# Sorted-block attention and its feed-forward: the first half of a hand-written order listed anew, one call per engine, with first keys in four PSUM tiles

## The chip, the core and the metric

One NeuronCore of a Trainium2 chip runs the whole program in one launch. The metric is the device time of that launch in microseconds (us). The engines named below are PE (TensorE, the matrix products; PEld is its loading of weights), DVE (VectorE), ACT (ScalarE), POOL (GpSimd) and SP (SyncE, which here only starts transfers). Each engine works through its own list of instructions in order. An instruction waits on semaphores until what it reads is written and what it overwrites is no longer needed, and all that stands behind it in the same list waits too. Transfers started from POOL run on a software queue (q0 in the profile), those started from SP on a hardware queue (q1).

## The reference, cut to what matters

```python
# q, k, v: (4, 8, 768, 64); sort_net: (4, 8, 8, 8); 8 blocks of 96 tokens
P = sort_net
for _ in range(5):                      # Sinkhorn rounds
    P = P - max(P, -1); P = exp(P)
    P = P / (sum(P, -1) + 1e-9); P = P / (sum(P, -2) + 1e-9)
k_sorted = einsum('bhij,bhjcd->bhicd', P, k_blocks)   # the same for v
scores = 1/8 * q_blocks @ k_sorted.T                  # block by block, 96 x 96
attn = exp(scores - max); attn /= sum(attn) + 1e-9
x = (attn @ v_sorted) as (3072, 512)
h = x @ w_in                                          # w_in (512, 2048)
out = (h * cos(h)) @ w_out                            # w_out (2048, 512)
```

## The kernel before

The work is cut into 8 chunks `n` of 384 tokens. A chunk is half of one batch entry: 4 blocks `u` of 96 tokens, all 8 heads. For each chunk the kernel turns the queries so that the head dimension lies on the partitions, multiplies them with the sorted keys (scores `sc`), takes the row maximum and subtracts it (DVE lines 492, 494, 824, 828), takes the exponential (ACT, line 573, into `p_buf`), turns the result (`pT`, by PE or by a DMA transpose from SP, line 591), multiplies with the sorted values (`av`, line 628), normalises (lines 639, 641) and turns into `xT`. Then comes the feed-forward: `up` (PE, line 672, 8 pairs of feature tiles in PSUM tiles `h`), cosine (ACT, line 676), gate `c * h` (DVE, line 680), and the output layer `down` (PE, line 697, PSUM tiles `o`), whose result is copied out and stored from SP (line 687).

The sorted keys and values come from products of the loaded `k`, `v` with block-diagonal matrices `bd`, `bdv` that are spread from the Sinkhorn result. Batches 0 and 1 are sorted at the beginning (`kp`, `v0`, `v_sort_b`), batches 2 and 3 in the middle (`k_sort_g`, `v_sort_g`). PSUM tiles come from two pools, `big` (handed on as `*B`) and `acc` (`*C`).

Nothing schedules the work: the order is a hand-written list of calls, and each call issues instructions on one or more engines. Each engine's list is the order in which these calls name it. `fill=` puts products of zeros (line 246) ahead of a call's own products on PE.

The transfers that matter below:

- `load_q(n)` starts from POOL. For n of 3 and more it is 8 transfers of 48 KB in pieces of 128 bytes (line 129), and `q_transpose_dma(n)` then turns them with two DMA transposes from SP into `q_turned` (line 149). Chunks 0 to 2 are turned by PE.
- `load_pair(vbuf, ...)`, z from 0 to 5, loads the values of batches 2 and 3 in six transfers of 256 KB from POOL (line 92). `v_permute` is a copy on POOL that reorders values (line 179).
- `p_hold(2, 2)` is a tiny copy on POOL that reads `pT` of block (2, 2), so that POOL waits there until that DMA transpose has landed (line 599). `hold_keys()` does the same for the swapped keys (line 429), `hold(q_turned[z])` for queries.
- `k_swap(kT[1])` moves sorted keys between partitions with two transfers from SP (lines 421, 422).

The first use of chunk 3's queries is `batch(("sc", 3, 0), ("ks", 1, A))`, a set of 8 score products (line 507) and 16 key products on PE.

Of the kernel before, what the change touches and what calls it, by code (L numbers as in the profile page):

```python
# [18 lines left out]
def kernel(  # L19
# [377 lines left out]
    blocks = [block([pick[:]])]  # L397
    spread(bds[0], blocks[0], xs=slice(H, 2 * H))

    def values_matrix():  # L400
        spread(bdv, blocks[1], xs=slice(0, H))
        spread(bds[0], blocks[0], xs=slice(0, H))
        spread(bdv, blocks[1], xs=slice(H, 2 * H))
# [197 lines left out]
    def p_hold(n, u):  # L601
        hold(pT[n, u])
# [14 lines left out]
    def av_products(n, u, fill=0):  # L617
# [5 lines left out]
        pt = pT.pop((n, u)).rearrange("p a c -> p (a c)")  # L623
# [270 lines left out]
    wz = iter(range(40, D, 4))  # L894
    kz = iter(range(6, 12))

    def k_next():
        k_sort_g(next(kz) * 4, A, *C)

    def w_next(eng=A, pool=None, tag="acc"):  # L900
        v_sort_g(next(wz), 4, eng, pool or acc, tag)

    kp(2, *B)
    kp(0, *B)
    v_permute(slice(0, 64), 32, False, 8, 40)
    v_permute(slice(0, 64), 40, False, 8, 48)
    v_permute(slice(0, 64), 48, False, 8, 56)
    v_permute(slice(0, 64), 56, False, 8, 64)
    k_place(2, A, 1)
    k_place(2, V, 0)  # L910
    kp(1, *B)
    k_place(0, A, 0)
    blocks.append(block([pick[:, :, z * PB:(z + 1) * PB] for z in (1, 0)]))
    k_place(1, V, 0)
    k_place(1, A, 1)
    values_matrix()
    k_place(0, A, 1)
    s_ps(0, 0, fill=3)
    v0(4, *C)
    s_max(0, 0)  # L920
    v0(0, *B)
    v0e(4, A)
    s_sub(0, 0)
    s_ps(0, 3)
    v0e(0, A)
    v0(5, *C)
    s_max(0, 3)
    load_w_out(0)
    v0e(5, A)
    s_ps(0, 1)  # L930
    load_w_out(1)
    load_w_out(2)
    load_w_out(3)
    v0(6, *C)
    ones(0)
    expo(0, 0, True)
    s_ps(0, 2)
    s_sub(0, 3)
    v0(1, *C)
    v0e(6, A)  # L940
    s_max(0, 1)
    expo(0, 3, True)
    v0(3, *B, fill=2)
    s_sub(0, 1)
    v0e(1, A)
    p_ps(0, 0, *C, fill=2)
    v0e(3, A)
    s_max(0, 2)
    v0(7, *C)
    expo(0, 1, True)  # L950
    kxp(2)
    v0(2, *B, fill=1)
    p_ev(0, 0, V)
    v0e(7, A)
    s_sub(0, 2)
    kxp(0)
    p_ps(0, 1, *C)
    v0e(2, A)
    p_ps(0, 3, *C)
    p_ev(0, 1, V)  # L960
    expo(0, 2, True)
    kxp(1)
    av_products(0, 0)
    z_turned(1)
    av_norm(0, 0, True)
    av_products(0, 1)
    p_ev(0, 3, A)
    p_ps(0, 2, *C)
    av_norm(0, 1, True)
    x_ps(0, 0, *B)  # L970
    load(kbuf, 0, kin_d[1])
    p_ev(0, 2, A)
    load(vbuf, 64, vin_d[1])
    picks(pick_pair, (2, 3))
    av_products(0, 3, fill=2)
    av_norm(0, 3, True)
    x_ps(0, 1, *C)
    x_ev(0, 0, A)
    av_products(0, 2)
    q_products(1, 0, 0, 16, *C)  # L980
    x_ev(0, 1, A)
    av_norm(0, 2, True)
    x_ps(0, 3, *B)
    q_place_half(1, 0, 1, A)
    up_four(0, 0, 0)
    z_vperm()
    up_four(0, 0, 1)
    x_ev(0, 3, V)
    q_place_half(1, 0, 0, V)
    up_four(0, 3, 0)  # L990
    up_four(0, 3, 1)
    z_turned(0)
    cos_four(0, 0)
    p_pads()
    up_four(0, 1, 0)
    cos_four(0, 3)
    gate_four(0, 0)
    x_ps(0, 2, *C)
    up_four(0, 1, 1)
    gate_four(0, 3)  # L1000
    up_four(0, 2, 0)
    cos_four(0, 1)
    up_four(0, 2, 1)
    x_ev(0, 2, V)
    gate_four(0, 1)
    up_four(1, 2, 0)
    cos_four(0, 2)
    up_four(1, 2, 1)
    gate_four(0, 2)
    up_four(1, 1, 0)  # L1010
    cos_four(1, 2)
    up_four(1, 1, 1)
    gate_four(1, 2)
    up_four(1, 3, 0)
    cos_four(1, 1)
    up_four(1, 3, 1)
    gate_four(1, 1)
    q_products(1, 1, 0, 16, *C)
    cos_four(1, 3)
    last = block([pick_pair[:]], *C)  # L1020
    q_place_half(1, 1, 0, V)
    up_four(1, 0, 0)
    q_place_half(1, 1, 1, A)
    gate_four(1, 3)
    up_four(1, 0, 1)
    s_ps(1, 1)
    spread(bds[1], last)
    cos_four(1, 0)
    s_ps(1, 0)
    s_max(1, 1)  # L1030
    down_four(0, 0)
    gate_four(1, 0)
    load_q(2)
    down_four(0, 1)
    load_pair(pair, kin_d, 0 * CD // 2, 1 * CD // 2)
    load_pair(pair, kin_d, 1 * CD // 2, 2 * CD // 2)
    v_permute(slice(64, 128))
    down_four(0, 2)
    s_sub(1, 1)
    down_four(1, 0)  # L1040
    s_max(1, 0)
    expo(1, 1, True)
    ks(5, *B)
# [211 lines left out]
```

## Time and profile before

| what | us |
|---|---|
| median of 3 runs | 232.06 (231.93 to 232.34) |
| the profiled execution | 231.61 |
| its span in the profile | 229.8 |
| PE busy | 220.8 (96%) |
| DVE, ACT, POOL busy | 170.8, 154.4, 96.1 |
| PE on the chain that ended last | 90% of the span |

The span runs from the first to the last instruction that the profile shows; 1.8 us of the profiled execution lie outside it. The chain that ended last is found by going back from the last instruction, at each step to what released it. An idle row such as `[12.68 <-DMA pT<-p_buf]` says how long the engine stood still just before that instruction, and what ended it. "DMA to landing" is the time from the issue of a transfer to its completion.

### The profile page before, as it was taken

To read this page: it belongs to the slowest core of one execution; us is meant where nothing else is said; L and a number is where in the kernel's file an instruction comes from. 1 tells how busy PE (TensorE), PEld (TensorE's weight loads), DVE (VectorE), ACT (ScalarE), POOL (GpSimd) and SP (SyncE) were. 2 spreads that over 40 slices of the span, in tenths; PEclk is the share of its full clock that TensorE was granted. 3 is DMA by queue.
4 is the path that set the end of the run, shared out by engine and by line. 5 is a ranking of instruction groups with operands and counts; after the bars stand their busy time and mean duration, and the time that the engine had idled before them with its cause. 6 is when DMAs were issued, how large, how long until landed. Compare 5 with 4: busy or idle time off the path is not lost.

```text
span 229.8 us, 5513 instructions
## 1 busy us (share of the span) xinstructions
PE 220.8 (96%) x2245; PEld 138.7 (60%) x2268; DVE 170.8 (74%) x291; ACT 154.4 (67%) x207; POOL 96.1 (42%) x121
## 2 busy tenths in 40 slices
PE   8788999999999999999999999999999999999994
PEld 3378898567765566655665456655655565556554
DVE  6769968978698778868489977987699769646700
ACT  5659877777889858797688466736674667716521
POOL 7999999399950197943609000800000000000000
PEclk9999999999999999999999999999999999999999
DMA  6999999994999799667979939964924440351012
GB/s 83 225 187 207 202 206 236 195 227 148 124 124 191 171 139 148 118 135 146 162 118 163 135 74 148 210 98 81 206 92 80 90 160 0 69 147 46 0 46 94
DMA packets 67833, 31.21 MB, mean 136 GB/s; under 512 B 56416, under 2 KB 63200, under 8 KB 67552
## 3 DMA queue, kind: packets, MB, share of 16 engines
q0 software_dynamic: 24048, 13.64, 43.3%
q1 hardware_dynamic: 43472, 17.02, 35.1%
q8 instruction: 18, 0.29, 0.5%
q10 hardware_dynamic: 288, 0.20, 0.3%
q14 instruction: 7, 0.06, 0.1%
HBM read 27.27 MB, written 6.29 MB: 146 GB/s over the span
## 4 chain that ended last, share of the span: by engine, by line
PE 90%; DVE 3%; POOL 2%; issue 1%; ACT 1%; POOLq 0%; ACTq 0%
PE h L672 32%; PE o L697 30%; PE h L860 5%; PE o L881 4%; PE av L628 4%; PE sc L441 3%; PE ks L408 2%; PE o L1219 2%; PE pps L838 1%; PE sc L507 1%; PE xps L659 1%; PE vs L785 1%; PE vs L452 1%; PE qps L268 1%; PE xps L847 1%
## 5 line engine op out<-in xcount | busy, mean ns | idle before, releaser
L672 PE MATMUL h<-xT,w_in_t 128*128 128x384 bf16 x448 | 78.4, 326 | 0.1
L697 PE MATMUL o<-w_out_t,gg 128*128 128x512 bf16 x303 | 73.7, 379 | 1.0 <-issue 0.3
L676 ACT ACTIVATE c<-h,half_pi 128x768 f32<-128x768 f32 x56 | 50.5, 902 | 26.0 <-PE h L672 25.0
L680 DVE TENSOR_TENSOR gg<-c,h 128x768 bf16<-128x768 f32 x56 | 52.7, 949 | 19.5 <-ACT c L676 19.5
L672 PEld LDWEIGHTS <-w_in_t 128*128 128x128 bf16 x448 | 42.2, 98 | 26.3 <-DVE xT L259 0.6
L697 PEld LDWEIGHTS <-gg 128*128 128x128 bf16 x320 | 29.0, 99 | 28.3
L573 ACT ACTIVATE p_buf<-s 96x768 bf16<-96x768 f32 x32 | 26.6, 843 | 5.2 <-DVE s L494 4.0
L179 POOL COPY vperm<-kv 64x768 bf16<-64x768 bf16 (+2 forms) x12 | 28.4, 2416 | 3.9 <-DMA kv<-in_v_dram 3.9
L494 DVE TENSOR_TENSOR s<-sc,mx 96x384 f32<-96x384 f32 (+1 forms) x33 | 24.3, 735 | 1.6
L492 DVE TENSOR_REDUCE mx<-sc 96x4 f32<-96x384 f32 (+1 forms) x33 | 24.0, 729 | 0.2 <-PE sc L507 0.2
L641 DVE TENSOR_TENSOR xn<-av,r 96x512 bf16<-96x512 f32 x32 | 22.0, 687 | 1.1
L129 POOL DMA_DIRECT2D kv<-in_q_dram x24 | 16.0, 676 | 0.7 <-issue 0.7
L257 ACT COPY kv<-o 128x512 f32<-128x512 f32 (+2 forms) x10 | 5.2, 524 | 14.1 <-PE o L697 11.5
L257 ACT CAST kTs<-ks 128x512 bf16<-128x512 f32 (+1 forms) x18 | 11.0, 630 | 5.3 <-PE ks L408 4.4
L639 DVE RECIPROCAL r<-av 96x8 f32<-96x8 f32 x32 | 6.4, 199 | 9.6 <-PE av L628 9.1
L129 POOL DMA_DIRECT2D q_mem<-in_q_dram x16 | 10.7, 687 | 2.0 <-DMA kv<-in_v_dram 1.5
L881 PE MATMUL o<-w_out_t,gg 128*128 128x512 bf16 x45 | 11.2, 379 | 0.2
L259 DVE COPY kv<-o 128x512 f32<-128x512 f32 (+1 forms) x5 | 3.1, 612 | 11.1 <-PE o L1219 8.5
L860 PE MATMUL h<-xT,w_in_t 128*128 128x192 bf16 x128 | 11.1, 246 | 0.0
L441 PE MATMUL sc<-kTs,q_turned 128*128 128x96 bf16 x152 | 11.1, 206 | 0.0
L599 POOL CAST held<-q_turned 96x1 f32<-96x1 bf16 x2 | 0.4, 184 | 24.3 <-DMA q_turned<-q_mem 16.3
L860 PEld LDWEIGHTS <-w_in_t 128*128 128x128 bf16 x128 | 10.5, 98 | 0.0
(134 smaller groups left out, 285.6 us busy)
## 6 DMA issues: line engine op xcount, KB each, us to landing
out_dram<-kv SPq DMA_DIRECT2D x12, 256.0 KB, 2.7
out_dram<-o_s SPq DMA_DIRECT2D x10, 256.0 KB, 3.5
w_in_t<-in_moe_w_in_dram POOLq DMA_DIRECT2D x4, 512.0 KB, 11.7
w_out_t<-in_moe_w_out_dram POOLq DMA_DIRECT2D x4, 512.0 KB, 12.3
kv<-in_k_dram POOLq DMA_DIRECT2D x2, 768.0 KB, 9.8
kv<-in_v_dram POOLq DMA_DIRECT2D x2, 768.0 KB, 12.9
pair<-in_k_dram POOLq DMA_DIRECT2D x2, 768.0 KB, 12.3
kv<-in_v_dram POOLq DMA_DIRECT2D x6, 256.0 KB, 5.3
```

The costliest lines, as they stand in the source:

```text
L129: nc.gpsimd.dma_start(out=q_heads[:, i, :, e], in_=src[:, ih * IC + i, :, e])
L179: nc.gpsimd.tensor_copy(dst, src)
L492: nc.vector.reduce_max(mx[:], scv, axis=AX.X)
L494: nc.vector.tensor_tensor(s, scv, mx.to_broadcast(list(s.shape)), op=ALU.subtract)
L573: nc.scalar.activation(p[:, :, :blk], s_t.pop((n, u)).rearrange("p e h c -> p (e h) c"), AF.Exp, scale=scale)
L641: nc.vector.tensor_tensor(xn.rearrange("p h e d -> p e h d"), avv[:, :, :, :D], r.to_broadcast([blk, 2, H2, D]), op=ALU.mult)
L672: nc.tensor.matmul(h[:, f2, :w], w_in_t[:, kk, f * 128:(f + 1) * 128], xT[n][:, kk], start=(kk == 0), stop=(kk == KC - 1))
L676: nc.scalar.activation(c[:], h[:, :, :w], AF.Sin, bias=half_pi[:, 0:1])
L680: nc.vector.tensor_tensor(gt[n, fp // 2][:, f:f + 2], c[:], h[:, :, :w], op=ALU.mult)
L697: nc.tensor.matmul(o[:], gt[n, f // 4][:, f % 4, ts * 128:(ts + 1) * 128], w_out_t[:, f, :], start=(f == 0), stop=(f == FC - 1))
L860: nc.tensor.matmul(o[:, part, f2 * w:(f2 + 1) * w], w_in_t[:, kk, f * 128:(f + 1) * 128], xT[0][:, kk, h * w:(h + 1) * w], start=(kk == 0) ...
L881: nc.tensor.matmul(out_ps[ts][:], gt[0, q][:, f % 4, ts * 128:(ts + 1) * 128], w_out_t[:, f, :], start=(f == 0), stop=(f == FC - 1))
```

## The change

Three helper changes, and one new list:

- The first keys `kp` go to four PSUM tiles of 16, 16, 8 and 8 (two in `big`, two in `acc`) in place of three of 16. All four spreads of the block-diagonal matrices come ahead of the keys. The column of ones of `vS[0]` is a memset on DVE, not on POOL.
- The products of zeros stand at other places: ahead of `s_ps` 2 in place of 3, of `v0` none in place of 3, of `av_products` 3 and 1 in place of 2, of `p_ps` 2 as before. The blocks of chunk 0 go in the order 1, 0, 2, 3.
- Calls that issued on several engines are split: `up` into `uh` (PE), `uc` (ACT), `ug` (DVE); score products and their reductions into `qs` and `qr`; sets of eight into `bt` and `be`; turned outputs into `xp`, `xe`; sorted keys and values into `kg`/`kge`, `vg`/`vge`, `vb`/`vbe`; the output layer into quarters `dn` and the copy `dc`.
- Everything from the first keys to the end of chunk 3's output layer is listed anew, flat, with these. From `q_transpose_dma(6)` on the program is the same.

```diff
-    blocks = [block([pick[:]])]
+    blocks = [block([pick[:]]), block([pick[:, :, z * PB:(z + 1) * PB] for z in (1, 0)])]
     spread(bds[0], blocks[0], xs=slice(H, 2 * H))
...
+    spread(bdv, blocks[1], xs=slice(0, H))
+    spread(bds[0], blocks[0], xs=slice(0, H))
+    spread(bdv, blocks[1], xs=slice(H, 2 * H))
+    nc.vector.memset(vS[0][:, :, D:D + 1], 1.0)
...
-        pt = pT.pop((n, u)).rearrange("p a c -> p (a c)")
+        pt = pT[n, u].rearrange("p a c -> p (a c)")
...
-    kp(2, *B)
-    kp(0, *B)
...
-    k_place(2, A, 1)
-    k_place(2, V, 0)
-    kp(1, *B)
...
-    s_ps(0, 0, fill=3)
...
+    kp(0, 16, *B)
+    kp(32, 16, *B)
+    kp(24, 8, *C)
+    k_place(0, V, 0)
+    k_place(32, A, 0)
...
+    kp(16, 8, *C)
...
+    s_ps(0, 1, fill=2)
...
-    zeros_between(3)
-    load_q(3)
-    hold_keys()
-    load_pair(vbuf, vin_d, 0 * CD // 6, 1 * CD // 6)
-    load_pair(vbuf, vin_d, 1 * CD // 6, 2 * CD // 6)
-    load_pair(vbuf, vin_d, 2 * CD // 6, 3 * CD // 6)
...
-    q_transpose_dma(3)
...
-    down(1, 1, 1, nc.sync, mid=[(expo, 2, 3, True)], late=[(av, 2, 0, True)])
-    batch(("sc", 3, 0), ("ks", 1, A))
-    p_hold(2, 2)
-    for z in range(3, 6):
-        load_pair(vbuf, vin_d, z * CD // 6, (z + 1) * CD // 6)
-    load_q(4)
-    v_permute(slice(0, 128))
...
+    uh(1, 3)
+    uc(1, 3)
+    ug(1, 0)
+    qs(2, 0, 1, *C)
+    qr(2, 0, 1)
+    ug(1, 3)
...
+    load_pair(vbuf, vin_d, 4 * CD // 6, 5 * CD // 6)
...
+    zeros_between(3)
+    uh(1, 4)
+    uh(1, 5)
...
+    p_pads()
+    uh(1, 6)
+    load_q(3)
...
+    load_pair(vbuf, vin_d, 1 * CD // 6, 2 * CD // 6)
...
+    q_transpose_dma(3)
...
+    load_pair(vbuf, vin_d, 3 * CD // 6, 4 * CD // 6)
+    dn(1, 1, 0)
+    load_pair(vbuf, vin_d, 2 * CD // 6, 3 * CD // 6)
...
+    load_pair(vbuf, vin_d, 0 * CD // 6, 1 * CD // 6)
+    bt(('sc', 2, 2), ('sc', 2, 3), ('ks', 0, A))
...
+    load_pair(vbuf, vin_d, 5 * CD // 6, 6 * CD // 6)
...
+    expo(2, 3, True)
+    load_q(4)
+    dn(1, 1, 3)
+    bt(('sc', 3, 0), ('ks', 1, A))
+    vb(1, 40, 8, *B)
+    vbe(1, 40, 8, A)
+    dc(1, 1, nc.sync)
+    be("ks", 1, A)
+    dn(1, 0, 2)
+    load_q(5)
+    dn(1, 0, 3)
+    dc(1, 0, 'held')
+    qr2(3, 0)
+    av_products(2, 0)
...
+    hold_keys()
+    p_hold(2, 2)
...
+    p_hold(3, 3)
```

What the diff of a list does not show is where each engine's rows now stand. Three places matter.

POOL, from the two loads of keys of batches 2 and 3 (`pair`) on. Of `load_q` the odd chunks write `kv`, the even ones `q_mem`. Before:

```order
L92 DMA pair<-in_k_dram 128x3072 x2
L179 COPY vperm<-kv 64x1536 x4
L137 MEMSET kv 96x16x64 x2
L129 DMA kv<-in_q_dram 96x4x64 x8
L429 CAST held<-kTs 128x1
L92 DMA kv<-in_v_dram 128x1024 x3
L137 MEMSET q_mem 96x16x64 x2
L599 CAST held<-pT 96x1
L92 DMA kv<-in_v_dram 128x1024 x3
L129 DMA q_mem<-in_q_dram 96x4x64 x8
L179 COPY vperm<-kv 128x1536 x4
```

The same stretch of POOL after the change:

```order
L179 COPY vperm<-kv 64x1536 x4
L92 DMA kv<-in_v_dram 128x1024
L137 MEMSET kv 96x16x64 x2
L742 MEMSET p_buf_107 96x8x32
L742 MEMSET p_buf_108 96x8x32
L742 MEMSET p_buf_109 96x8x32
L129 DMA kv<-in_q_dram 96x4x64 x8
L92 DMA kv<-in_v_dram 128x1024 x5
L129 DMA q_mem<-in_q_dram 96x4x64 x8
L129 DMA kv<-in_q_dram 96x4x64 x8
L179 COPY vperm<-kv 128x1536 x2
```

One load of values and the three memsets `p_buf` (`p_pads`) moved ahead of `load_q(3)` (the first `kv<-in_q_dram`). The two waits `held` stood between `load_q(3)` and the other loads; they now come behind all of the rows above, so that five loads of values, `load_q(4)` and `load_q(5)` follow `load_q(3)` directly.

SP, its first transfers, before. The two transposes `q_turned_95<-kv` are `q_transpose_dma(3)`, `pT<-p_buf` are those of chunk 2's exponentials:

```order
L687 DMA out_dram<-o_s 128x512 x2
L687 DMA out_dram<-c 128x512
L421 DMA kTs<-kTs 64x1536
L422 DMA kTs<-kTs 64x1536
L149 DMA_TRANSPOSE q_turned_95<-kv 128x16x96 x2
L591 DMA_TRANSPOSE pT<-p_buf_109 128x8x96
L591 DMA_TRANSPOSE pT<-p_buf_107 128x8x96
L591 DMA_TRANSPOSE pT<-p_buf_108 128x8x96
```

SP after:

```order
L686 DMA out_dram<-o_s 128x512
L686 DMA out_dram<-c 128x512
L420 DMA kTs<-kTs 64x1536
L421 DMA kTs<-kTs 64x1536
L686 DMA out_dram<-o_s 128x512
L149 DMA_TRANSPOSE q_turned_95<-kv 128x16x96 x2
L590 DMA_TRANSPOSE pT<-p_buf_109 128x8x96
L590 DMA_TRANSPOSE pT<-p_buf_107 128x8x96
L590 DMA_TRANSPOSE pT<-p_buf_108 128x8x96
```

The key swap moved ahead of the third store; the transposes kept their order, and the chunk's queries still go ahead of `pT`.

DVE, from the first spread of the block-diagonal matrix to the first scores, before:

```order
L393 TENSOR_TENSOR bd_151<-maskp,bl 128x64
L259 CAST kTs<-ks 128x2x4x4x16 x2
L393 TENSOR_TENSOR bdv<-maskp,bl 128x64
L393 TENSOR_TENSOR bd_151<-maskp,bl 128x64
L393 TENSOR_TENSOR bdv<-maskp,bl 128x64
L824 TENSOR_REDUCE mx<-sc 96x8
```

DVE after:

```order
L393 TENSOR_TENSOR bd_151<-maskp,bl 128x64
L393 TENSOR_TENSOR bdv<-maskp,bl 128x64
L393 TENSOR_TENSOR bd_151<-maskp,bl 128x64
L393 TENSOR_TENSOR bdv<-maskp,bl 128x64
L402 MEMSET vS 96x128
L259 CAST kTs<-ks 128x2x4x4x16
L259 CAST kTs<-ks 128x2x4x4x8
L259 CAST kTs<-ks 128x2x4x4x16
L823 TENSOR_REDUCE mx<-sc 96x8
```

The spreads and the memset moved ahead of the copies of the first keys, and there are three copies, one of them half as wide, in place of two.

More of the change, by code (lines that the diff above doesn't have):

```diff
@@ L936 @@
[L936 to L963, printed above, removed]
@@ L985 @@
[L985 to L1009, printed above, removed]
@@ L1010 @@
[L1010 to L1031, printed above, removed]
@@ new lines @@
+    up_four(1, 2, 1)
+    s_ps(1, 1)
+    kse(1, A)
+    z_turned(0)
+    load_w_out(2)
+    cos_four(1, 2)
+    ks(3, *C)
+    load(vbuf, 64, vin_d[1])
+    kse(3, A)
+    up_four(1, 1, 0)
+    up_four(1, 1, 1)
+    down_four(0, 0)
+    down_four(0, 1)
+    s_max(1, 1)
+    s_sub(1, 1)
+    gate_four(1, 2)
+    cos_four(1, 1)
+    gate_four(1, 1)
+    z_turned(1)
+    s_ps(1, 2)
+    s_max(1, 2)
+    s_ps(1, 3)
+    expo(1, 0, True)
+    down_four(0, 2)
+    p_ps(1, 0, *B)
+    s_sub(1, 2)
+    s_max(1, 3)
```

701 lines of the change are left out of this document (515 added, 186 removed).

## The prediction

> **What bounds the kernel now.** I read first the page's busy times and its chain that ended last.
>
> ```profile
> PE 220.8 (96%) x2245; PEld 138.7 (60%) x2268; DVE 170.8 (74%) x291; ACT 154.4 (67%) x207; POOL 96.1 (42%) x121
> PE 90%; DVE 3%; POOL 2%; issue 1%; ACT 1%; POOLq 0%; ACTq 0%
> ```
>
> The products of PE set the time, and no other engine is near it. Next I asked where PE stands still: busy times by stretch (us from:to, its length, then busy us of PE, PEld, DVE, ACT, POOL, PE's granted clock, DMA share, GB/s).
>
> ```profile
> 12.00:20.00 8.00, 7.02 (x176) 5.99 (x178) 5.87 (x11) 5.35 (x10) 7.63 (x8) 1.00 1.19 202
> 20.00:28.00 8.00, 7.54 (x132) 6.80 (x132) 7.59 (x14) 7.10 (x12) 7.68 (x13) 1.00 1.30 204
> 28.00:54.00 26.00, 25.84 (x322) 20.07 (x323) 20.21 (x31) 19.34 (x25) 22.18 (x23) 1.00 1.11 217
> 54.00:66.00 12.00, 12.00 (x175) 8.38 (x172) 9.96 (x18) 10.29 (x15) 11.90 (x17) 1.00 0.87 111
> ```
>
> Between 12 and 28 us PE idles 0.98 + 0.46 = 1.44 us; between 28 and 66 us 0.16 us. So a new order can win only in the start. It can lose wherever it lets something arrive late, and a DMA share about 1 says that the transfers run without a gap. So I then read the transfers: POOL in order of time, and SP.
>
> ```profile
> 44.40 11.29 POOL L179 COPY vperm<-kv 64x1536 bf16<-64x1536 bf16 x4 [3.50 <-DMA kv<-in_v_dram]
> 55.76 1.83 POOL L137 MEMSET kv<- 96x1024 bf16 x2
> 57.54 5.34 POOL L129 DMA_DIRECT2D kv<-in_q_dram  x8
> 63.06 1.64 POOL L92 DMA_DIRECT2D kv<-in_v_dram  x3
> 79.23 0.18 POOL L599 CAST held<-pT 96x1 f32<-96x1 bf16 x1 [12.68 <-DMA pT<-p_buf]
> 79.68 1.59 POOL L92 DMA_DIRECT2D kv<-in_v_dram  x3 [0.27 <-issue]
> 81.25 4.81 POOL L129 DMA_DIRECT2D q_mem<-in_q_dram  x7
> ...
> 65.01 6.50 SPq L149 DMA_TRANSPOSE q_turned<-kv  x2
> 72.65 4.82 SPq L591 DMA_TRANSPOSE pT<-p_buf  x3
> ```
>
> POOL issues `load_q(3)` from 57.54 to 62.88 and three loads of values behind it. It then stands 12.68 us on `p_hold(2, 2)`, until a transpose of chunk 2 has landed, and only then issues the other three loads and `load_q(4)`. Look at what this idle time does: chunk 3's queries are turned in the quiet that it makes. Their two transposes, and the three loads:
>
> ```profile
> L149 SPq DMA_TRANSPOSE q_turned<-kv x2: 1632/3154/4677, 65.0 to 66.8; - x2
> DMA to landing us min/median/max: 6.7/6.9/7.1
> ...
> L92 POOL DMA_DIRECT2D kv<-in_v_dram x3: 551/556/561, 63.1 to 64.2; - x3
> DMA to landing us min/median/max: 4.4/5.7/6.5
> ```
>
> The transposes land at 65.0 + 7.1 = 72.1 and 66.8 + 6.7 = 73.5; the last load at 64.2 + 6.5 = 70.7. From the chain that ended last, a stretch of the output layer and the first use of those queries:
>
> ```profile
> 72.11 2.48 PE o L697 x11
> ...
> 77.87 0.28 PE sc L507 x8
> ```
>
> A margin of 4.4 us. Now the packets by queue in 66:70 (first two rows; loads of values beside the transposes), 70.5:73.5 (one row; transposes alone) and 86:89.2 (two rows; `load_q(4)` beside another transpose and a store).
>
> ```profile
> q0 software_dynamic: 329, 0.58, 98.7%
> q1 hardware_dynamic: 257, 0.07, 10.0%
> ...
> q1 hardware_dynamic: 2619, 0.65, 101.8%
> ...
> q0 software_dynamic: 1975, 0.27, 135.7%
> q1 hardware_dynamic: 757, 0.20, 54.4%
> ```
>
> Beside loads of values q1 got 257/4 = 64 packets per us, and the loads moved 0.58 MB in 4 us, so one of 256 KB takes 1.8 us. Alone, q1 got 2619/3 = 873 per us or more. Beside `load_q(4)` it got 757/3.2 = 237 per us against 617 of q0.
>
> **The change, part by part.** *Chunk 3's queries* are the term that decides. POOL's 11.29 us of copies wait for a load that lands at 44.40; the same bytes stand ahead of it after the change. From there POOL has one load of values (0.55), the zeros (1.83) and the three memsets of `p_pads`:
>
> ```profile
> L743 POOL MEMSET p_buf<- x3: 313/313/318, 38.2 to 38.7; 96x256 bf16 x3
> ```
>
> which are 0.9. `load_q(3)` is thus issued from 44.4 + 11.3 + 0.55 + 1.83 + 0.9 = 59.0 to 64.3, 1.4 us later than before, and the transposes from 66.4 (65.01 + 1.4). Behind `load_q(3)` on q0 now stand five loads of values, not three, and then at once `load_q(4)`, whose issue no longer waits for `p_hold(2, 2)`. The loads end at 70.7 + 1.4 + 2 x 1.8 = 75.7. Until then the transposes get some 64 x 9.3 = 600 packets. They need 3072 (two transposes of 16 x 96 rows), so 2470 remain, and `load_q(4)` has as many (8 pieces of 384) ahead of it on the other queue. The late end: 237 per us while q0 gives out 3072 at 617 per us (5.0 us, 1180 packets), the remaining 1290 at 873 (1.5 us), landing at 82.2. The early end, with nothing beside them: 2470/873 = 2.8, landing at 78.5. `load_q(4)` is issued from about 67 on, well before 75.7, so the late end is nearer; the last pieces wait for loads to land and come behind, which brings it forward a little. I take 81.5.
>
> By the Trainium skill (DMA: Bandwidth & Descriptors, Queues, rings and completion order) each DMA engine goes round-robin between the queue rows that have work, packet by packet. An equal share of the 237 + 617 = 854 per us would give 2470/427 = 5.8 us and a landing at 81.5; the shares 257 to 329 beside loads of values agree with it, those of 237 to 617 don't, and the sum goes by the rows.
>
> When does PE want them? With the trace's mean for every form of product, 147.7 us of products stand from `bt(('sc', 3, 0), ...)` to the end of the new order, and 146.2 us from the same call in the old one. Mostly, two quarters of `dn` went behind it (2 x 4 products of 2.48/11 = 0.225, 1.8 us). So a kernel as far along as before reaches it at 77.9 - 1.5 = 76.4, and with the small stalls below at 77.5 to 78. At 81.5 it is 81.5 - 76.4 = 5.1 us behind; all of PE's list stands behind that call. How early PE comes doesn't matter, for the transposes hang on POOL and q0 alone: what the start wins is lost in this wait.
>
> *Behind it* the transposes `pT` follow on the same SP queue. `expo(2, 3)` needs the buffer that the first of them reads, so ACT takes it 0.9 us after the queries land (768 packets at 873), and five ACT calls that PE soon needs stand behind it: estimated 0.5 us more (0 to 1).
>
> *The start.* The bounds are 0 and the 1.44 us of idle, with some 0.4 us for two fewer products of zeros on top. I find the first scores about 0.6 us earlier, since the spreads no longer stand behind copies of keys. But `s_ps(1, 0)` now follows the first `up_four` by 2.5 us of PE's work, while its queries need a cosine and three copies, two on ACT and one on DVE:
>
> ```profile
> L866 ACT ACTIVATE c<-h,half_pi 128x768 f32<-128x768 f32 x3 | 2.6, 902 | 0.6 <-PE h L860 0.6
> L257 ACT COPY q_turned<-qps 64x768 bf16<-64x768 bf16 x1 | 0.8, 794 | 0.3 <-PE qps L268 0.3
> ...
> L259 DVE COPY q_turned<-qps 64x768 bf16<-64x768 bf16 x1 | 0.6, 550 | 0.0
> ```
>
> That is 0.90 + 2 x 0.79 + 0.55 = 3.0 us, with handing on some 3.1: 0.6 us lost again. I take 0.25 us won, in the case that the queries come in time; otherwise nothing.
>
> *The key swap* is issued at about 51 us in place of 56.4, behind two stores:
>
> ```profile
> L687 SPq DMA_DIRECT2D out_dram<-o_s x2: 333/350/368, 45.6 to 49.0; - x2
> DMA to landing us min/median/max: 6.0/7.4/8.8
> ...
> L421 SPq DMA_DIRECT2D kTs<-kTs x1: 540/540/540, 56.4 to 56.4; - x1
> DMA to landing us min/median/max: 2.8/2.8/2.8
> ```
>
> Both stores landed at 54.4 to 55.0, when the loads had ended. The swap cannot be much ahead: 56 to 56.6 (between 51 + 2.8 and 51 + 8.8 = 59.8), while PE wants it at about 55.5 in `qs(2, 1, 1)`. Stall 0.8 us (0 to 2).
>
> *DVE ahead of `uh(1, 5)`.* That call takes the PSUM tile that `ug(1, 3)` reads, and DVE reaches the end of `ug(1, 3)` after three score halves, two gates and two copies:
>
> ```profile
> L680 DVE TENSOR_TENSOR gg<-c,h 128x768 bf16<-128x768 f32 x56 | 52.7, 949 | 19.5 <-ACT c L676 19.5
> L494 DVE TENSOR_TENSOR s<-sc,mx 96x384 f32<-96x384 f32 (+1 forms) x33 | 24.3, 735 | 1.6
> L492 DVE TENSOR_REDUCE mx<-sc 96x4 f32<-96x384 f32 (+1 forms) x33 | 24.0, 729 | 0.2 <-PE sc L507 0.2
> ```
>
> 3 x (0.735 + 0.729) + 2 x 0.95 + 1.3 = 7.6 us against 6.9 us of PE's products: stall 0.6 us (0 to 0.8). Both small stalls only make PE wait less for the queries, and count when these are in time. `load_q(5)` now waits for chunk 3's transposes and holds the copies `v_permute` behind it on POOL. They then end at about 94 to 102 us, and PE wants them from 96 on: nothing, with at most 1 us lost. The holds that moved back, the memset given to DVE (0.7 us on POOL) and the transfers after 90 us cost nothing: POOL idles 12.68 us before, and the calls that read these come later.
>
> *Sum.* 231.61 (profiled) + 5.1 + 0.5 = 237.2. The median of the runs lies 0.45 above that profiled execution, so 237.7.
>
> **The rivals.** *In time after all.* If the transposes win against `load_q(4)`, they land at 78.5, about when PE comes; what remains are the small stalls, -0.25 + 0.8 + 0.6, up to +3 when they slip by 1 or 2 us. That gives 232.8 to 235.2, taken 233.5. For it: 2619 packets in 3 us once q0 is empty. Against it: POOL has nothing left that holds `load_q(4)` back.
>
> *Faster.* The start is the mechanism: scores 0.6 us earlier, two products of zeros fewer, and PE's idle time filled. It decides if the queries land before PE comes (about 76.2 then, since PE has not stalled) and the two stalls are under 0.3 us together. The most that it can give is 1.44 + 0.4, so 230.2 to 231.6. Against it stands that 75.7 is already the end of the loads ahead.
>
> *No change.* Start and small stalls cancel, the queries in time: 231.6 to 232.5.
>
> *Late and cold.* A wait of 4 us on PE is new; the longest that I find behind the first transfers is 1.23 us (first row). At the start, after idling, the first nine products of zeros (up to 4.6 us) went slower than the next six (from 4.7 us):
>
> ```profile
> 9.33 0.53 PE L323 MATMUL qps<-ident,q_mem 96*64 96x96 bf16 x16 [1.23 <-ACT q_turned L329]
> ...
> L246 PE MATMUL idle<-warm 128*128 128x512 bf16 x9 | 4.0, 631 | 1.0 <-DVE warm L231 1.0
> L246 PE MATMUL idle<-warm 128*128 128x512 bf16 x6 | 1.8, 439 | 0.0
> ```
>
> If that comes back after the wait, nine products lose 4.0 - 9 x 0.3 = 1.3 us: 239.0. The Trainium skill (TensorE: Matmul & The Clock Gate, Part 1) has such a rule: after an idle window of about 3.4 us the clock falls to half, and recovers after as long a time of work. The last two rows agree in kind, though the clock column reads 1.00 there, and no row of before shows it after a later idle.
>
> **How the numbers follow.** Late queries 0.66 (235.2 to 240), of which late and cold 0.12; in time with small stalls 0.14; no change 0.07; faster 0.13. About 0.2%, 0.46 us, is what a measurement can tell from no change. The first two are slower: 0.80; same 0.07; faster 0.13. The range leaves out the last two and goes from 232.8 to 240.5, the late end of the transposes (82.2) with 1 us behind it and the cold products.
>
> **What would show it.** In the changed profile: the transposes of line 149 issued near 66.4 with over 12 us to landing; PE idle 3 to 4.5 us ahead of line 506 at 77 to 82, released by that DMA; q0 without a gap from 44 to 80 us; POOL without the 12.68 us. Scores at about 15 us and the first `up_four` before 27 us would show the start right. I am wrong if the transposes land within 10 us of issue, if `load_q(4)` is issued after 72 us, or if PE comes to line 506 only after 80 us.

## The result: 11 us slower, and the profile after

| | before | after |
|---|---|---|
| median of the runs, us | 232.13 (231.88 to 232.34, 6 runs) | 243.09 (241.5 to 245.06, 6 runs) |
| ratio | | 1.0476, 95% interval 1.0425 to 1.0526 |
| the profiled execution, us | 231.61 | 243.12 |
| span, us | 229.8 | 241.3 |
| mean granted clock of PE | 1.000 | 0.986 |

The forecast was 237.7, between 232.8 and 240.5, so the measured time lies outside it. It had the sign, the place and the transfer right, and half of the size. Busy times and the chain that ended last, from the page of the changed kernel:

```profile
PE 223.8 (93%) x2266; PEld 140.0 (58%) x2266; DVE 174.6 (72%) x295; ACT 153.6 (64%) x206; POOL 94.7 (39%) x120
PE 58%; POOL 18%; DMA 14%; issue 4%; SPq 2%; DVE 1%; ACT 1%; POOLq 0%; DVEq 0%; ACTq 0%
```

PE was 90% of that chain before and is 58% now; POOL and transfers hold a third of it. Where PE stands still shows in the busy times by stretch (same columns as in the prediction; the granted clock is the third number from the end):

```profile
54.00:66.00 12.00, 10.33 (x97) 6.69 (x96) 8.14 (x14) 7.83 (x12) 11.66 (x16) 1.00 0.73 123
66.00:78.00 12.00, 12.00 (x138) 7.27 (x135) 10.77 (x14) 10.40 (x14) 8.02 (x14) 1.00 1.20 148
78.00:90.00 12.00, 4.77 (x42) 2.45 (x41) 2.12 (x3) 3.02 (x5) 4.40 (x8) 0.72 1.48 149
```

From 54 to 66 us PE idles 1.7 us; from 78 to 90 us it idles 7.2 us and works at a mean clock of 0.72. PE in order of time, the instructions that waited, and the output layer behind the wait:

```profile
57.69 0.33 PE L440 MATMUL sc<-kTs,q_turned 128*128 128x96 bf16 x4 [1.67 <-DMA kTs<-kTs]
...
80.90 0.21 PE L506 MATMUL sc<-kTs,q_turned 64*128 64x96 bf16 x1 [2.60 <-DMA q_turned<-kv]
85.74 0.50 PE L506 MATMUL sc<-kTs,q_turned 64*128 64x96 bf16 x7 [4.63 <-DMA q_turned<-kv]
...
87.05 3.23 PE L996 MATMUL o<-w_out_t,gg 128*128 128x512 bf16 x8
```

The three numbers to keep: 1.67 us on the key swap, 2.60 + 4.63 = 7.2 us on the two halves of chunk 3's queries, and 3.23 us for eight products of the output layer. POOL and SP in order of time say why:

```profile
46.30 11.19 POOL L179 COPY vperm<-kv 64x1536 bf16<-64x1536 bf16 x4 [6.50 <-DMA kv<-in_v_dram]
...
60.91 5.34 POOL L129 DMA_DIRECT2D kv<-in_q_dram  x8
66.22 2.70 POOL L92 DMA_DIRECT2D kv<-in_v_dram  x5
68.86 2.85 POOL L129 DMA_DIRECT2D q_mem<-in_q_dram  x4
...
68.73 10.59 SPq L149 DMA_TRANSPOSE q_turned<-kv  x2
79.48 5.93 SPq L590 DMA_TRANSPOSE pT<-p_buf  x3
```

As forecast, the 12.68 us of POOL's idling are gone, five loads of values and `load_q(4)` follow `load_q(3)` at once, and the transposes are issued (68.73) at the same time as `load_q(4)` (68.86). PE is released by them at 80.9 and 85.7.

### The profile page after: what moved, and what is told of

It is laid out like the page before. It is cut to its first block, busy times and chain, and to the rows that moved or that the text cites. A ratio compares the mean times of both kernels' runs of the same rounds, so it can differ in the third digit from the quotient of the medians.

```text
span 241.3 us, 5541 instructions
## 1 busy us (share of the span) xinstructions
PE 223.8 (93%) x2266; PEld 140.0 (58%) x2266; DVE 174.6 (72%) x295; ACT 153.6 (64%) x206; POOL 94.7 (39%) x120
## 4 chain that ended last, share of the span: by engine, by line
PE 58%; POOL 18%; DMA 14%; issue 4%; SPq 2%; DVE 1%; ACT 1%; POOLq 0%; DVEq 0%; ACTq 0%
PE h L671 17%; PE o L696 16%; PE o L996 9%; PE h L898 8%; POOL vperm L179 7%; DMA q_turned<-kv 6%; DMA kv<-in_v_dram 5%; PE av L627 2%; PE sc L440 2%; DMA out_dram<-o_s 2%; POOL kv L129 2%; DMA kv<-in_q_dram 2%; PE o L1540 1%; POOL w_out_t L164 1%; POOL q_turned L142 1%
## 5 line engine op out<-in xcount | busy, mean ns | idle before, releaser
L671 PE MATMUL h<-xT,w_in_t 128*128 128x384 bf16 x256 | 43.2, 326 | 0.0
L696 PE MATMUL o<-w_out_t,gg 128*128 128x512 bf16 x176 | 41.1, 379 | 0.0
L996 PE MATMUL o<-w_out_t,gg 128*128 128x512 bf16 x144 | 35.9, 390 | 0.0
L671 PEld LDWEIGHTS <-w_in_t 128*128 128x128 bf16 x256 | 24.7, 98 | 16.2
L898 PE MATMUL h<-xT,w_in_t 128*128 128x384 bf16 x192 | 33.3, 326 | 0.6 <-DMA xT<-xn 0.3
L491 DVE TENSOR_REDUCE mx<-sc 96x4 f32<-96x384 f32 (+1 forms) x33 | 24.0, 729 | 11.5 <-PE sc L506 8.5
L696 PEld LDWEIGHTS <-gg 128*128 128x128 bf16 x176 | 16.2, 98 | 16.5
L898 PEld LDWEIGHTS <-w_in_t 128*128 128x128 bf16 x192 | 18.3, 98 | 12.1 <-issue 0.5
L996 PEld LDWEIGHTS <-gg 128*128 128x128 bf16 x144 | 13.3, 102 | 13.3 <-issue 1.6
L638 DVE RECIPROCAL r<-av 96x8 f32<-96x8 f32 x32 | 6.3, 198 | 11.2 <-PE av L627 11.1
L257 ACT CAST kTs<-ks 128x512 bf16<-128x512 f32 (+2 forms) x17 | 9.8, 596 | 5.9 <-PE ks L407 5.9
```

What stands on the lines that cost most here:

```text
L491: nc.vector.reduce_max(mx[:], scv, axis=AX.X)
L671: nc.tensor.matmul(h[:, f2, :w], w_in_t[:, kk, f * 128:(f + 1) * 128], xT[n][:, kk], start=(kk == 0), stop=(kk == KC - 1))
L696: nc.tensor.matmul(o[:], gt[n, f // 4][:, f % 4, ts * 128:(ts + 1) * 128], w_out_t[:, f, :], start=(f == 0), stop=(f == FC - 1))
L898: nc.tensor.matmul(h[:, f2, :TC], w_in_t[:, kk, f * 128:(f + 1) * 128], xT[n][:, kk], start=(kk == 0), stop=(kk == KC - 1))
L996: nc.tensor.matmul(out_ps[n, ts][:], gt[n, q][:, f % 4, ts * 128:(ts + 1) * 128], w_out_t[:, f, :], start=(f == 0), stop=(f == FC - 1))
```

## The experiments

The theory: the time is lost where POOL's loads meet the DMA transposes; the cold clock and the key swap add to it. The rival: the new order of PE, ACT and DVE costs it.

**Chunk 3's queries without load_q(4) beside them.**

```diff
+    hold(q_turned[1])
+    nc.gpsimd.tensor_copy(held[:blk], q_turned[1][:blk, 1, :1])
     load_q(4)
     ...
-    load_q(5)
     ...
     v_permute(slice(0, 128), 16, True, 16, 32)
+    load_q(5)
```

> The changed kernel, but POOL waits (two tiny copies that read both halves of chunk 3's turned queries) before it issues load_q(4), and load_q(5) goes behind the four copies v_permute that follow. The five loads of values ahead stay. Theory (the transposes are late because load_q(4) shares the DMA engines with them): the loads still end at about 77.4 us, the rest of the transposes then runs alone at about 1000 packets per us and lands near 80.3; PE, there at 78.3, waits 2 us in place of 7.5, too short for the cold clock (1.7 us). Time 243.1 - 5.4 - 1.7 = 236.0, between 234.5 and 237.5. Rival (the five loads, or the transposes' own pace, make them late, and load_q(4) doesn't matter): 241.5 to 244.

Measured: ratio 1.0316 (1.0257 to 1.0375), median 239.5. PE's waits in its profile:

```profile
79.36 0.21 PE L506 MATMUL sc<-kTs,q_turned 64*128 64x96 bf16 x1 [0.51 <-DMA q_turned<-kv]
82.21 0.50 PE L506 MATMUL sc<-kTs,q_turned 64*128 64x96 bf16 x7 [2.63 <-DMA q_turned<-kv]
```

The queries land 3.5 us earlier (82.2 in place of 85.7), and the median falls by 3.6 us, into neither of the two ranges. The profiled execution (240.61) is the slowest of the four and only 2.5 us below that of the change: the clock stayed at 0.50 for 5.5 us of work behind the queries (82.2 to 87.7), 4.0 in the change. So `load_q(4)` matters, which the rival denied; but the queries still land 2 us later than I expected (80.3), and the mean clock (0.984) is no better.

**Two loads of values fewer ahead of them, too.**

```diff
     # as above, and:
-    load_pair(vbuf, vin_d, 0 * CD // 6, 1 * CD // 6)
     ...
-    load_pair(vbuf, vin_d, 5 * CD // 6, 6 * CD // 6)
     ...
     nc.gpsimd.tensor_copy(held[:blk], q_turned[1][:blk, 1, :1])
+    load_pair(vbuf, vin_d, 0 * CD // 6, 1 * CD // 6)
+    load_pair(vbuf, vin_d, 5 * CD // 6, 6 * CD // 6)
     load_q(4)
```

> As e1_hold, and two of the five loads of values (the first and the last sixth) also go behind the two holding copies, so that three stand ahead of the transposes as in the kernel before. Theory: the loads ahead end near 74.2 us, the transposes land near 77.4, before PE comes at 78.3, so no wait on chunk 3's queries and no cold clock: 243.1 - 7.5 - 1.7 = 233.9, between 232.8 and 235. What is left above the kernel before is the wait of about 1.8 us on the key swap. Rival (something else in the new list costs several us): above 236.

Measured: ratio 1.0332 (1.0268 to 1.0396), no better than the run before and in the rival's range (above 236). PE's waits:

```profile
79.25 0.34 PE L506 MATMUL sc<-kTs,q_turned 64*128 64x96 bf16 x7 [1.10 <-DMA q_turned<-kv]
85.17 0.43 PE L627 MATMUL av<-vS,pT 96*128 96x65 bf16 x8 [2.37 <-DMA pT<-p_buf]
```

The queries are another 3 us earlier, but now chunk 2's `pT` is late by 2.37 us: POOL is let go as soon as the queries have landed, and issues two loads of values at 79.80 us and `load_q(4)` from 80.85, while SP has issued the next three transposes from 75.85 to 80.6 and they have yet to land. So what is lost here, too, has to do with POOL's order; that these loads delay `pT` is read from the times, not tested by itself. The kernel before let POOL go only on `pT(2, 2)`, the last of the three. The one wait that looked like idle time kept the way free for five transposes.

**The cold clock.**

```diff
             if kind == "sc":
                 ps["q", x[0], x[1]] = o
+                if x == [3, 0]:
+                    keep_warm(28, o[:, 0])
                 by_half(*x, o)
```

> The changed kernel with 28 products of zeros (28 x 0.216 = 6.0 us at full clock) on PE directly ahead of the products that wait for chunk 3's queries; they write the PSUM tile that those products overwrite. Transfers are as they were. Theory (after 7.5 us of idling PE's clock is halved, and the products behind it lose about 1.7 us): the wait is filled, the clock stays at 1.00, and the time is 243.1 - 1.7 = 241.4 (240.8 to 242). Rival (the products behind the wait are slow for want of data or weights): 243.1, unchanged. If the products of zeros outlast the wait they cost up to 0.5 us.

Measured: 241.08, ratio 1.0387 (1.0355 to 1.0419), mean clock 1.000 in its profile. The products of zeros, the end of the wait, and the same eight products of the output layer:

```profile
77.53 6.26 PE L246 MATMUL sc<-warm 128*128 128x512 bf16 x27
...
84.32 0.34 PE L506 MATMUL sc<-kTs,q_turned 64*128 64x96 bf16 x7 [0.39 <-DMA q_turned<-kv]
...
85.08 1.89 PE L998 MATMUL o<-w_out_t,gg 128*128 128x512 bf16 x8
```

Eight products take 1.89 us in place of 3.23. Products that compute nothing make the kernel 2.0 us faster. In the two profiled executions (240.16 against 243.12) 1.4 of the 3.0 us are queries that landed earlier (84.3 against 85.7), so about 1.5 us is the clock. By the rows, from the end of the wait to the end of these eight products, it is 4.5 us in place of 2.7 (85.74 to 90.28, 84.32 to 86.97): 1.9 us, of which not all reaches the end. The time course of the clock in the changed kernel, by shorter stretches:

```profile
80.00:82.00 2.00, 0.21 (x1) 0.09 (x1) 0.00 (x0) 0.00 (x0) 0.59 (x1) 1.00 2.41 123
84.00:85.70 1.70, 0.00 (x0) 0.00 (x0) 0.00 (x0) 0.00 (x0) 0.00 (x0) 0.50 1.69 201
88.00:89.00 1.00, 1.00 (x4) 0.34 (x3) 0.29 (x1) 1.00 (x2) 0.69 (x2) 0.50 1.28 81
90.00:92.00 2.00, 2.00 (x38) 1.43 (x35) 1.36 (x4) 1.38 (x2) 1.96 (x3) 1.00 1.12 131
```

Full clock until about 83 us, half of it to the end of the wait and on through 4 us of work, full again at 90. The Trainium skill (TensorE: Matmul & The Clock Gate, Part 1) says so: half clock after an idle window of about 3.4 us, and about as long a time of work to come back. This trace agrees with it, where the kernel before could not show it. But the clock can also fall after less: in the first of the three runs with POOL's protection put back (below) it fell behind a wait of 1.67 us (108.3 to 110.0), and PE was busy for half of the 3.4 us before the fall.

```profile
107.80:111.25 3.45, 1.73 (x48) 1.25 (x47) 2.57 (x4) 0.93 (x2) 3.45 (x6) 1.00 1.23 111
111.30:114.60 3.30, 3.30 (x16) 1.65 (x16) 1.18 (x3) 2.01 (x3) 2.50 (x4) 0.50 1.43 189
```

**The same transfers in the kernel before.** If the order of PE, ACT and DVE is not to blame, moving POOL's wait alone must do harm.

```diff
-    p_hold(2, 2)
     for z in range(3, 6):
         load_pair(vbuf, vin_d, z * CD // 6, (z + 1) * CD // 6)
     load_q(4)
     v_permute(slice(0, 128))
+    p_hold(2, 2)
```

> The kernel before with one line moved: p_hold(2, 2), the wait of POOL for a transpose of chunk 2, goes from ahead of three loads of values and load_q(4) to behind them and the copies v_permute. All lists but POOL's stay. Theory: six loads of values and load_q(4) now run ahead of or beside chunk 3's transposes, which land at 82.5 to 84 in place of 73.5; PE wants them at 77.9 and waits 4.6 to 6 us, with the cold clock 1.7 more: 238.4 to 240. Rival (the loss comes from the new order on PE, ACT and DVE, and PE would find other slack): 232 to 234.

Measured: ratio 1.069 (1.0666 to 1.0713), six runs from 244.2 to 250.7, all above both ranges; the profiled one is the longest of them, so its waits are the upper end. PE's wait, SP's issue of the two transposes, and the packets by queue from 78 to 82 us:

```profile
94.10 0.65 PE L628 MATMUL av<-vS,pT 96*128 96x65 bf16 x8 [16.82 <-DMA pT<-p_buf]
...
65.85 19.13 SPq L149 DMA_TRANSPOSE q_turned<-kv  x2
...
q0 software_dynamic: 339, 0.17, 64.2%
q1 hardware_dynamic: 357, 0.09, 58.7%
```

One moved line costs more than the whole change. 0.26 MB in 4 us is 65 GB/s: both queues have work, and the DMA engines move three tenths of what the transposes move alone (0.65 MB in 3 us before, 217 GB/s). My sum of turns and shares had a wait of 4.6 to 6 us here; it can't describe this. Two runs take it apart. First the loads of values early, `load_q(4)` still held:

```diff
     for z in range(3, 6):
         load_pair(vbuf, vin_d, z * CD // 6, (z + 1) * CD // 6)
+    p_hold(2, 2)
     load_q(4)
```

> The kernel before with p_hold(2, 2) moved one step only, from ahead of the last three loads of values to behind them; load_q(4) still waits. Six loads of values then stand on the queue ahead of chunk 3's transposes. Theory (in e4_before_nohold the DMA engines fell to some 70 to 100 GB/s from 71 to 86 us while values and transposes were both under way): the slow mix stays, queries land after 80, 240 to 246. Rival (load_q(4) made e4 slow, values only take their turn of 1.7 us each): loads end at 76, queries land at 79, PE waits 1 to 1.5 us: 233 to 234.5.

Then `load_q(4)` early, the loads of values still held:

```diff
+    load_q(4)
     p_hold(2, 2)
     for z in range(3, 6):
         load_pair(vbuf, vin_d, z * CD // 6, (z + 1) * CD // 6)
-    load_q(4)
```

> The kernel before with load_q(4) moved ahead of p_hold(2, 2); the last three loads of values still wait. Chunk 3's transposes then meet load_q(4) but only three loads of values. Theory (the mix with values is the slow one): the loads of values end at 70.7 as before, then both queues share 850 packets per us, queries land at 77.5 to 79.5, PE waits 0 to 2 us: 232 to 234.5. Rival (the mix with load_q(4) is the slow one): queries land after 80, 237 or more.

Measured: 243.7 (ratio 1.0473, 1.0418 to 1.0528) with the values, 237.3 (1.0233, 1.0207 to 1.026) with the queries of chunk 4. PE's wait and SP's issue in each, the first two rows with values (the profiled execution, 241.08, is the fastest of the four), the last three with queries:

```profile
83.89 0.65 PE L628 MATMUL av<-vS,pT 96*128 96x65 bf16 x8 [6.71 <-DMA pT<-p_buf]
65.66 12.52 SPq L149 DMA_TRANSPOSE q_turned<-kv  x2
...
80.31 0.43 PE L628 MATMUL av<-vS,pT 96*128 96x65 bf16 x8 [3.15 <-DMA pT<-p_buf]
65.61 6.69 SPq L149 DMA_TRANSPOSE q_turned<-kv  x2
72.84 6.59 SPq L591 DMA_TRANSPOSE pT<-p_buf  x3
```

The mix with loads of values costs more, 11.5 us against 5.1, but it also has twice the bytes (768 KB against 384), so that one piece is worse than the other is not shown. I had given the queries 0 to 2 us, and they cost 5, as the rival of that run had it. The issue on SP itself stretches: for the two transposes of the queries 12.5 us with values and 19.1 with both, 6.5 before; with `load_q(4)` alone it stays at 6.7, and the three `pT` behind it take 6.59 in place of 4.82. So chunk 2's `pT` comes later in all three: in the old order that is what PE meets first.

**The loads of `w_out` apart.**

```diff
     load_w_out(0)
+    load_w_out(3)
+    load_w_out(1)
+    load_w_out(2)
```

> The changed kernel with the four loads of w_out issued one behind the other again (the second to fourth moved up to the first on POOL). Theory: in the changed kernel the load queue ran dry at 26 to 29 us, and everything behind it came 1.9 us later; with the queue fed, the values of batch 1 land at 44.4 in place of 46.3, chunk 3's queries land 1.9 us earlier, and the key swap's wait of 1.5 us shrinks below 0.5 but gains nothing, since the wait for the queries swallows it: 243.1 - 1.9 = 241.2, between 240 and 242.2. Rival (the 1.9 us have another cause): 242.5 to 244.

Measured: 241.42, ratio 1.0406 (1.0383 to 1.0429). First the cause. Up to 31 us the load queue q0 of the changed kernel is not behind (1.45 MB from 24 to 31 us, 1.41 before). From 32 to 36 us it is; q0 of the changed kernel, of the one before, and of this run:

```profile
q0 software_dynamic: 736, 0.74, 116.0%
q0 software_dynamic: 752, 0.88, 127.3%
q0 software_dynamic: 821, 0.82, 123.3%
```

In the changed kernel POOL issued the first load of `w_out` at 24.70 us and the second only at 29.05; before, all four were out at 22.7, here at 27.95. This run's rows:

```profile
45.16 11.25 POOL L179 COPY vperm<-kv 64x1536 bf16<-64x1536 bf16 x4 [5.15 <-DMA kv<-in_v_dram]
...
56.95 0.33 PE L440 MATMUL sc<-kTs,q_turned 128*128 128x96 bf16 x4 [0.35 <-DMA kTs<-kTs]
...
84.94 0.50 PE L506 MATMUL sc<-kTs,q_turned 64*128 64x96 bf16 x7 [4.65 <-DMA q_turned<-kv]
```

The median falls by 1.7 us, as expected (1.9). In the profiled execution (241.67) the copies start 1.1 us earlier, not 1.9, and the queries land 0.8 earlier; in the last two kernels below, which issue `w_out` two and two, the copies start at 44.57 and 44.69. The wait for the key swap shrinks from 1.67 to 0.35, and nothing of that is gained on top: the wait for the queries swallows it.

**POOL's protection put back, three times.** The first try also moved two copies `v_permute` ahead of `load_q(4)`:

```diff
     # behind load_q(3): three loads of values, then
+    hold_keys()
+    p_hold(2, 2)
+    load_pair(vbuf, vin_d, 0 * CD // 6, 1 * CD // 6)
+    load_pair(vbuf, vin_d, 5 * CD // 6, 6 * CD // 6)
     v_permute(slice(0, 128), 32, True, 16, 48)
     v_permute(slice(0, 128), 48, True, 16, 64)
+    load_q(4)
```

> The changed kernel with POOL's protection put back: three loads of values behind load_q(3), then hold_keys and p_hold(2, 2), then two loads of values, the first two copies v_permute, load_q(4), the other copies, and load_q(5) last; and the loads of w_out together as in e5_feed. PE, ACT, DVE and SP keep the order of the change. Theory (the whole loss lies in how POOL's transfers meet the transposes, and the key swap): queries land near 76, before PE wants them at 77; chunk 2's transposes run alone; what is left is 0.8 us of the start and up to 1 us of small waits: 233.3, between 232.2 and 235. Rival (the new order of PE, ACT and DVE costs several us by itself): 236 or more.

Measured: ratio 1.0279 (1.0226 to 1.0333). It missed its 233.3, with four runs from 237.6 to 241.75, all in the rival's range (236 or more). In the profiled execution (241.39) PE waited 1.2 us on the queries (78.96), 2.6 and 0.9 us for copies and 1.7 for chunk 4's queries that I had moved behind them. PE asks for such a copy at 92.9 us there (95.52 - 2.61); in the kernel before it first reads one at 98.58. The second try took POOL's order of before as it was:

```diff
     load_w_out(0)
+    load_w_out(3)
     ...
+    p_pads()                 # ahead of load_q(2)
     ...
     zeros_between(3)
     load_q(3)
+    hold_keys()
     load_pair(...)           # three
+    zeros_between(4)
+    p_hold(2, 2)
     load_pair(...)           # three
     load_q(4)
     v_permute(...)           # four, in order
     load_q(5)
     ...
     vge(48, A)
+    vg(60, *C)               # moved from some 50 calls ahead,
+    vge(60, A)               # with vg(56), vge(56)
```

> The changed kernel with POOL's list, from the fourth quarter of the first copies v_permute on, in the order of the kernel before: zeros and load_q(3) first, hold_keys, three loads of values, the zeros for load_q(4), p_hold(2, 2), three loads of values, load_q(4), the four copies v_permute in order, load_q(5). The memsets of p_pads go ahead of load_q(2), two loads of w_out are issued where one was, and the two products sets vg(60) and vg(56), which want the last copy, go behind vg(48). The rest of PE, ACT, DVE and SP keeps the order of the change. Theory (the loss lies in how POOL's transfers meet the transposes): load_q(3) is issued from 58 us, queries land near 74.5 before PE wants them at 77, chunk 2's transposes run alone, no cold clock; what is left is the start's 0.8 us and small waits: 233.0, between 232.2 and 234.5. Rival (the new order of the other engines costs several us by itself): 236 or more.

Measured: 236.69, ratio 1.0194 (1.0178 to 1.021): above the theory's range (to 234.5) and just inside the rival's (236 or more), so this run alone doesn't clear the new order of PE, ACT and DVE. No row of it waits for chunk 3's queries any more, and the clock is 1.000, but new waits have come:

```profile
111.77 0.43 PE L627 MATMUL av<-vS,pT 96*128 96x65 bf16 x8 [0.82 <-DMA pT<-p_buf]
115.89 2.77 PE L898 MATMUL h<-xT,w_in_t 128*128 128x384 bf16 x16 [0.85 <-DMA xT<-xn]
129.01 0.50 PE L440 MATMUL sc<-kTs,q_turned 128*128 128x96 bf16 x8 [1.43 <-DVE gg L910]
```

The last wait stood behind the products that I had moved. So a third version has only these elsewhere:

```diff
     av_norm(3, 1, False)
+    vg(60, *B)
+    vge(60, A)
     ...
     dn(2, 0, 1)
+    vg(56, *B)
+    vge(56, A)
```

> As e9_pool_as_before, with the two product sets vg(60) and vg(56) at another place: behind av_norm(3, 1) and dn(2, 0, 1) and in the PSUM pool big, some 20 us earlier than there. In e9 PE waited 1.4 us at 129 us for a gate behind them. If that wait is of my own making, it goes and the time falls to about 235.3 (234.8 to 236); what is left of e9's 4.6 us then belongs to the new order of the other engines. If the wait belongs to the new order, the time stays at 236.7 (236.2 to 237.2).

Measured: 234.6, ratio 1.0118 (1.0096 to 1.0139), a little below the 234.8 to 236 expected if the wait was of my own making. The three rows above are gone; from 54 us on its waits are

```profile
56.48 0.33 PE L440 MATMUL sc<-kTs,q_turned 128*128 128x96 bf16 x4 [0.43 <-DMA kTs<-kTs]
79.94 0.67 PE L627 MATMUL av<-vS,pT 96*128 96x65 bf16 x16 [0.25 <-ACT vS L257]
81.33 0.41 PE L627 MATMUL av<-vS,pT 96*128 96x65 bf16 x8 [0.34 <-ACT kTs L257]
108.31 0.40 PE L971 MATMUL vs<-bd,vperm 128*128 128x128 bf16 x4 [1.01 <-DVE s L493]
```

With POOL's transfers put back, 8.5 of the 11.0 us are back too, though PE, ACT and DVE keep nearly all of the new order. Of the 2.5 us that are left, and that the new order may cost, 2.0 are these waits; the other 0.5 I can't tie to a row.

**The first keys alone, in the kernel before.**

```diff
-    kp(2, *B)
-    kp(0, *B)
...
+    kp(0, 16, *B)
+    kp(32, 16, *B)
+    kp(24, 8, *C)
     ...
+    kp(16, 8, *C)
     # and the spreads and the memset of ones ahead, as in the change
```

> The kernel before with the change's first keys alone: four PSUM tiles of 16, 16, 8 and 8, both block-diagonal products and all four spreads ahead of the keys, the column of ones as a memset on DVE. Everything from the first scores on keeps the order of before. Theory (in the changed kernel the first scores came 0.45 us earlier and the first input layer 1.2 us, and its loss of the start came later, at the scores of chunk 1): the scores come 0.4 us earlier and 0.2 to 0.6 us of it reach the end, 231.7, between 231.3 and 232.0. Rival (the chain behind the scores takes it back): 232.0 to 232.4.

Measured: 232.04 against 232.14, ratio 0.9997 (0.9989 to 1.0006, 12 runs): no change, as the rival had it. The first scores come at 15.27 us (15.52 before), and nothing of that arrives.

```profile
15.27 0.40 PE L803 MATMUL sc<-kTs,q_turned 64*128 64x64 bf16 x16
```

None of these kernels beats the one before by more than a measurement can tell.

## Why the prediction was half right

Followed along PE (each product counted with the mean time that its form takes in the kernel before, products of zeros left out, 20 products without a record in the trace before added from their weight loads), each time against the moment at which the kernel before had as much work left, the changed kernel is about 0.8 us ahead at 29 us, level within 0.3 from 33 to 54, 2.0 behind after the key swap, 1.8 when it comes to chunk 3's queries, 9.3 when the second half of them has landed, 10.1 after that set of products, and 11.2 at 90 us. From there on it stays between 10.4 and 11.8 and ends at 11.5 (243.12 - 231.61).

- *What bounds it, and that the start can win little*: right. First scores at 15.1 us, first `up_four` at 26.35, both as forecast. From 29 to 33 us, where `s_ps(1, 0)` stands, 0.8 to 0.9 us were lost where I had 0.6, so the start ends about level, not ahead by 0.25. The keys alone are worth nothing.
- *The key swap*: 1.67 us of waiting, in the range of 0 to 2; 0.8 was the guess. *DVE ahead of `uh(1, 5)`*: forecast 0.6, no wait there. As said, neither counts while the queries are late.
- *PE comes at 77.5 to 78*: 78.3. *The call is 1.5 us of products further on than in the old order*: right, for the kernel before had as much work left at 76.4. At the landing PE is then 85.7 - 76.4 = 9.3 us behind, where the sum had 5.1.
- *The queries land at 81.5*: this is the step that failed; they landed at 85.7. Its terms: "the same bytes stand ahead" was true, but not that they come as early: values landed at 46.30 in place of 44.40, 1.9 us. The runs that issue `w_out` together show this term: the copies then start at 45.16, 44.57 and 44.69. 0.4 us more went between the last issue of `load_q(3)` and the transposes (68.73 against 66.4 + 1.9). The remaining 1.9 us arose while the transposes ran, where the sum was wrong in more than one term. The packets of q0 in 66:69 of the kernel before (first row; q1 had none), by queue in 73:78, 78:79.5 and 81.5:82.7 of the changed one, and last of q1 in 78:79 of the old order with `load_q(4)` early (q0 had none):

```profile
q0 software_dynamic: 246, 0.44, 105.8%
...
q0 software_dynamic: 966, 0.63, 90.7%
q1 hardware_dynamic: 888, 0.23, 38.7%
...
q0 software_dynamic: 646, 0.08, 81.3%
q1 hardware_dynamic: 628, 0.16, 79.6%
...
q1 hardware_dynamic: 68, 0.02, 56.8%
q0 software_dynamic: 71, 0.01, 46.2%
...
q1 hardware_dynamic: 31, 0.01, 28.9%
```

  I had misread the row of 66:70. Its 257 packets all fall behind 69 us: the first packet of the transposes moved 4.25 us after their issue (4.39 in the changed kernel), and then they went faster than 64 per us. Neither that rate nor the equal share that I saw in 257 to 329 holds. By 78 us, the sum's 75.7 and the 2.3 us that all came later, 888 packets had moved, not 600. Beside `load_q(4)` (78:79.5) both queues got the same, 419 per us in place of 237. Right in these two terms, the sum would have had the queries earlier still. Two things made them later. From 81.5 to 82.7 us nearly nothing moved on either queue (68 and 71 packets, 22 GB/s). That is no matter of the mix: the last row has it with q1 alone at work, and the kernel before had it from 74.6 to 75.6 us (46 packets, on q1 alone), when its queries had landed. In these three, as in every profile of this case, it comes about 1 us behind a single packet of 16 KB on a queue q8, called `instruction` (at 80.6, 77.2 and 73.6 us); that this packet causes it is not shown. And up to the landing q1 moved 3937 packets (68.7 to 85.7 us), where it had moved 3136 before (65 to 73.5): some 800 of the `pT` transposes, which stand behind on the same queue, must have gone ahead of the last of the queries'.

  The equal share of 646 to 628 agrees with the rule that the prediction cited from the Trainium skill (DMA: Bandwidth & Descriptors, Queues, rings and completion order) better than with the 237 to 617 that I took from a row whose window held times with one queue at work. What neither had is the stretch of 1.2 us at 22 GB/s, and the slow ones of 4 us and more in the variants of the old order. I had summed packets as if the engines' rate were kept in any mix. It is not.
- *Late and cold*: had a chance of 0.12 and came true, with 1.5 to 1.9 us (1.3 forecast). It should have been in the sum of the late case: a wait of 4 us was the forecast itself, and the rows and the rule given there both speak for a cold clock after such a wait. The half us behind the queries (`expo(2, 3)`) can't be told apart from it.
- *In time after all* did not come, so its price is not tested. With the queries in time by another order of POOL the two kernels above took 236.69 and 234.6, against 232.8 to 235.2 (taken 233.5) in that rival.

Sum of the miss in the profiled executions, 11.5 against 5.6: 4.2 us in the landing (9.3 against 5.1), 1.4 behind it up to 90 us (1.9, by the rows the clock, where the sum had 0.5), and 0.3 from there to the end.

What stays open: what in the DMA engines makes the mix of the old order's variants so slow. The traces show that it happens where transposes and loads of 2-KB pieces are under way together, that SP's issue stretches with it, and that the time varies between executions (244 to 251 us in one kernel). Open, too, is why nearly nothing moves for about 1 us behind the packet on q8; had that fallen behind the landing, as in the kernel before, the queries would have come earlier by up to 1.2 us of the 1.9 (an estimate from the length of the stretch).

## What to carry to other kernels

An engine that idles on a wait of its own may be what keeps a shared resource free; before such a wait is moved, ask what will be issued earlier and what it then meets. Where transfers of two queues overlap, don't add up packets at the rate that each has alone: measure the mix. A critical wait hides the smaller ones behind it, so count them again when it is gone; and an idle time of PE of several us can cost its clock on top.

## What the runs showed of the hardware that I had not expected

- DMA transposes beside other loads can fall to three tenths of the rate that they have alone: 65 GB/s over 4 us with both queues at work, against 217. In the old order 768 KB of values beside them cost 11.5 us, 384 KB of queries in 128-byte pieces 5.1.
- The first packet of the transposes of chunk 3's queries moved 4.25 us after its issue with loads of values under way on the other queue, that of chunk 4's 1.17 us after its issue (at 92.88 us) with that queue empty; both in the kernel before.
- About 1 us behind a single 16-KB packet on the `instruction` queue q8, the other queues nearly stop for 1.0 to 1.2 us in the three profiles above, also with one of them at work alone.
- The issue of a DMA transpose on SP can take 17 us (19.13 us for two), and holds everything behind it on SP.
- PE's clock fell to 0.50 some 5 us after PE went idle (but for one product at 80.9 us) and stayed there for about 4 us of work. In another run it fell after a wait of 1.67 us.
- 28 products of zeros in a wait made the kernel 2.0 us faster.
